# Fourier mixing and a SoLU layer on one core: the down products of two units' signs as seven block products

## The chip, the core and the metric

The kernel runs on one core of a Trainium2 chip. The core has a matrix engine, TensorE (PE in the profile; PEld is its loading of weights), a vector engine (DVE), a scalar engine for activation functions (ACT), a general engine (POOL, GpSimd) and a queue engine that issues transfers (SP). They run side by side and wait for each other by semaphores. PE writes its results to PSUM, which has eight banks; all other data lie in SBUF. All data are 32-bit floats, and each such matmul shows in the profile as two passes, each with its own load of weights.

The metric is the time of one execution in device microseconds. The profile is of one execution.

## The reference

```python
X = np.fft.fft(x, axis=1)            # x: (8, 3136, 256)
X = np.fft.fft(X, axis=2)
x = X.real.reshape(25088, 256)

h = x @ w_in                          # (25088, 1024)
e = np.exp(h - max(h))                # by row
solu = h * e / (sum(e) + 1e-9)
ln = (solu - mean(solu)) / np.sqrt(var(solu) + 1e-6) * g_ln
out = ln @ w_out                      # (25088, 256)
```

## The kernel before

**Units.** The sequence transform of length 3136 = 49 x 64 is done in two stages. Two batches make a pair, so there are four pairs; k1 runs over 25 of the 49 frequencies of the first stage, since the others are mirrors. A unit (L214) is one k1 of one pair, 128 tokens, and with it their 128 mirror tokens: these are its two signs. Units with k1 = 0 have one sign. There are 100 units, 96 of them with two.

**A step** of the loop (L617) begins unit i and ends unit i - 4 (`lag`). It issues, for unit i: `up` (L222), two matmuls of 512 columns for the even and two for the odd part of h; `even` (L230, DVE) adds the middle term to the even part; `join` (L236, DVE) makes h of sign 0 from the even and the odd part, then h of sign 1 from h of sign 0, each with its row maximum; `expo` (L245, ACT) the exponentials u; `product` (L254, DVE) u times h; `square` (L261, ACT) the sum of squares about the mean; `turn_blocks` (L290, DVE) transposes u by blocks of 32; `stats` (L268, POOL) the factor rs of each token from the variance. Every second step `move_blocks` (L312) issues 16 transfers on the SP queue, which place the blocks of two units so that uT is their full transpose. The buffers of uT are two, each for two units.

For unit i - 4 the step issues `down` (L321), for each sign eight matmuls that add up a 128 x 1024 by 1024 x 256 product in PSUM: the stationary operand is a chunk of uT, whose signs lie alternately in memory, the moving one is 256 columns of Wo. `scale` (L328, ACT) multiplies by rs on the way to SBUF and `store` (L332) writes it out, sign 0 from the SP queue, sign 1 by an indirect transfer of POOL's.

For unit i + 2 it issues `transform2` (L189, PE), `take2` (L203, ACT, a copy to q) and `spread` (L207, SP, one row of q to r).

**The next pair** is prepared in the same steps: `load` (L101, SP and POOL), `add_mirror` (L126, POOL), `fold` (L134, DVE and ACT), `transform1` (L145, PE, then a copy on ACT and a transfer by `keep`, L178, on SP) and `turn` (L181, four transfers on POOL each), which brings a fifth of the pair's k1 back in another layout. `START` (L494) says in which steps; the transforms come at k1 from 4 to 19, the turns at 20 to 24. The last pair's steps have none of these.

**Order.** Every instruction stands on its engine's queue in the order in which the program issues it (`manual_schedule`, L519); no scheduler moves it. The first four units (`whole`) are transposed on PE instead (L295). PSUM holds two tiles of two banks each for `up` and four banks, taken in turn under one tag (`ps_m`, L77), for everything else.

Of the kernel before, what the change touches and what calls it, by code (L numbers as in the profile page):

```python
# [35 lines left out]
def kernel(  # L36
# [34 lines left out]
    gpool = ctx.enter_context(tc.tile_pool(name="gpool", bufs=6))  # L71
# [5 lines left out]
    ps_m = ctx.enter_context(tc.tile_pool(name="ps_m", bufs=4, space=PSUM))  # L77
# [5 lines left out]
    Wo = const.tile([P, KF, D], FP32, name="Wo")  # L83
    ones = const.tile([P, P], FP32, name="ones")
# [7 lines left out]

    class Pair:
        def __init__(self, p):
            self.p = p
            self.raw, self.y, self.y0 = {}, {}, None
            self.g, self.zs = {}, {}
# [45 lines left out]
    def transform1(pr, s):  # L145
# [6 lines left out]
        if l == 0:  # L152

            if pr.p or c < 2:
                pr.z = zpool.tile([ZR, CH, D], FP32, tag="z", name="z")
            elif c < 4:
                z = fpool.tile([P, FF], FP32, tag="u", name="z_u", bufs=2)
                pr.z = z[0:ZR].rearrange("p (l d) -> p l d", l=CH)
            else:
                pr.z = gpool.tile([P, KG, D], FP32, tag="g", name="z_g")[0:ZR, 0:CH, :]  # L160
            pr.zs[c] = pr.z
        y = pr.y[c]
        ps = ps_m.tile([P, 2, D], FP32, tag="m", name="ps1")
        if s == NH // 2 - 1:
            parts = [(ps[0:ZR, 0], y[:, l], 0), (ps[0:ZR, 1], pr.y0[:, 0], 1), (ps[0:ZR, 1], y[:, l + 1], 2)]
        else:
            parts = [(ps[0:ZR], y[:, l : l + 2], 0)]
        first = True
# [20 lines left out]
    def transform2(pr, k1):  # L189
# [6 lines left out]
        ps = ps_m.tile([P, KD * P], FP32, tag="m", name="ps2")  # L196
# [39 lines left out]
    def join(t, ps):  # L236

        t.nmax = small.tile([P, 2], FP32, tag="nmax", name="nmax")
        for s in t.signs:
            t.h[s] = fpool.tile([P, FF], FP32, tag="h", name="h", bufs=2)  # L240
            nc.vector.tensor_tensor_reduce(out=t.h[s], in0=t.h[0] if s else t.ev, in1=ps,  # L241
                                           scale=1.0 if s else -0.5, scalar=-3.0e38, op0=ALU.add, op1=ALU.max,
                                           accum_out=t.nmax[:, s : s + 1])

    def expo(t):  # L245
        t.esum = small.tile([P, 2], FP32, tag="esum", name="esum")
        t.neg = small.tile([P, 2], FP32, tag="neg", name="neg")
        for s in t.signs:
            nc.scalar.mul(out=t.neg[:, s : s + 1], in_=t.nmax[:, s : s + 1], mul=-1.0)  # L249
            t.u[s] = fpool.tile([P, FF], FP32, tag="u", name="u", bufs=2)  # L250
            nc.scalar.activation(out=t.u[s], in_=t.h[s], func=ACT.Exp, bias=t.neg[:, s : s + 1],  # L251
                                 accum_out=t.esum[:, s : s + 1])
# [15 lines left out]
    def stats(t):  # L268

        n = slice(0, len(t.signs))  # L270
        es = small.tile([P, 2], FP32, tag="es", name="es")
        nc.gpsimd.tensor_scalar(out=es[:, n], in0=t.esum[:, n], scalar1=1e-9, scalar2=1e-3,  # L272
                                op0=ALU.add, op1=ALU.mult)
        es2 = small.tile([P, 2], FP32, tag="es2", name="es2")
        nc.gpsimd.tensor_tensor(out=es2[:, n], in0=es[:, n], in1=es[:, n], op=ALU.mult)
        v = small.tile([P, 2], FP32, tag="v", name="v")
        nc.gpsimd.tensor_scalar(out=v[:, n], in0=t.ssq[:, n], scalar1=float(FF) ** -3, scalar2=None, op0=ALU.mult)  # L277
        nc.gpsimd.tensor_tensor(out=v[:, n], in0=v[:, n], in1=es2[:, n], op=ALU.add)
# [16 lines left out]
    def turn_whole(t):  # L295
# [4 lines left out]
        for s in t.signs:  # L300
            for half in range(2):
                ps = ps_m.tile([P, n, P], FP32, tag="m", name="ps_t")
# [17 lines left out]

    def down(t, s):  # L321
        uT = t.batch.uT[:, t.w].rearrange("p c i (n s) -> p c (i n) s", s=2)
        ps = ps_m.tile([P, D], FP32, tag="m", name="ps_o")
# [28 lines left out]
    mantissa = const.tile([P, NW], I32, name="mantissa")  # L352
    limits = const.tile([P, 3], FP32, name="limits")
# [12 lines left out]
    def exponent(w, raw):  # L366
# [3 lines left out]
        unit = qpool.tile([P, NW], I32, tag="unit", name="unit", bufs=3)  # L370
# [38 lines left out]
    class Weights:  # L409
# [72 lines left out]
        def centre(self):  # L482

            cs = ps_m.tile([P, D], FP32, tag="m", name="cs")
# [25 lines left out]
    def ahead_pe(pr, step):  # L510
# [5 lines left out]
        if 0 <= step - 20 < NK // KG:  # L516
            turn(pr, step - 20)

    with tc.manual_schedule():  # L519
# [24 lines left out]
        for i, limit in enumerate((-896.0, 255.0, 255.0 * 2.0 ** 23)):  # L544
            nc.vector.memset(limits[:, i : i + 1], limit)
# [56 lines left out]
        def begin(i):  # L602

            cur = units[i]
            if i % 2 == 0:
                batches.append(Batch(i >= whole))
            cur.batch, cur.w = batches[-1], i % 2
            even(cur, up(cur, 0))
            cur.odd = up(cur, 1)
            if i + 2 < len(units):  # L610
                nxt = units[i + 2]
                take2(nxt, transform2(pairs[nxt.p], nxt.k1))
                spread(nxt)
# [3 lines left out]
        for i in range(len(units) + lag):  # L617
            cur = units[i] if i < len(units) else None
            old = units[i - lag] if i >= lag else None
            ahd = pairs[cur.p + 1] if cur and cur.p + 1 < NP else None  # L620
            last = i >= len(units) - 2
            prv = units[i - 1] if 0 < i <= whole else None
            if i > lag:
                store(units[i - lag - 1])
            if cur and i > whole:
                begin(i)
            if prv:
                turn_whole(prv)
            if cur:
                join(cur, cur.odd)  # L630
# [3 lines left out]
            if cur:  # L634
                expo(cur)
            if ahd:
                ahead_pe(ahd, cur.k1)
            if old:
                order = old.signs[::-1] if old is units[-1] else old.signs
                ps_o = [down(old, s) for s in order]  # L640
            if i == 0:

                weights.narrow_out(3)
            if cur:
                for s in cur.signs:
                    product(cur, s)
                    if i < whole and s == 0:
                        square(cur, s)
                if i == 1:
                    weights.centre()  # L650
                if i < whole:

                    begin(i + 1)
                for s in cur.signs:
                    if i >= whole or s:
                        square(cur, s)
                    if i >= whole:
                        turn_blocks(cur, s)
            if old:
                scale(old, order[0], ps_o[0])  # L660
            if cur:
                if last:
                    move_blocks(batches[-1], slice(cur.w, cur.w + 1), (nc.sync, nc.gpsimd) if cur.w else (nc.sync,))
                elif cur.w and i >= whole:
                    move_blocks(batches[-1], slice(0, 2))
                stats(cur)
            if i == 0:
                turn(first, 1, nc.sync)
            elif i in (5, 8, 11):
                turn(first, (i + 1) // 3)  # L670
            if ahd:
                ahead(ahd, cur.k1)
            if old and 1 in old.signs:
                scale(old, order[1], ps_o[1])
        store(units[-1])
# [76 lines left out]
```

## Time and profile before

| | |
|---|---|
| time, three runs | 1188.86, 1189.22, 1191.11 us; median 1189.22 |
| profiled execution | 1191.11 us, its span 1189.0 us |
| granted TensorE clock | 1.000 of full |
| down products, L325 | 3136 passes of 128x256, mean 379 ns; 56% of the chain |
| up products, L227 | 800 passes of 128x512, mean 593 ns; 28% of the chain |
| second transform, L199 | 400 passes of 128x128, mean 274 ns; 4% of the chain |
| weight loads of L325, L199 | mean 196 and 191 ns |
| DMA | 16 engines, mean 156 GB/s |
| SP: 16 moves of uT (L319), every second step | 128 KB each |

How to read it: the profile's times of single matmuls include a tail that the next one overlaps, so their pitch is read from the chain of waits or from a group's length. The page's chain follows the work that ended last back from the end of the kernel; its shares say which engine's work was on that path. In a timeline the first column is the start from the beginning of the span, the second the length, and brackets give the idle time of the engine before the instruction and what ended it. In a list of groups the numbers behind the bar are the busy time of all, the mean of one in ns, and the idle time before them. Lines of a helper can stand for many places.

### The profile page before, as it was taken

How to read it: one execution, taken by the hardware profiler on the slowest of the kernel's cores; microseconds unless marked ns; L12 is line 12 of the kernel's file. 1: busy time of each engine (PE TensorE's matmuls, PEld its weight loads, DVE VectorE, ACT ScalarE, POOL GpSimd, SP SyncE). 2: the span in 40 equal slices, each digit the busy share in tenths (PEclk: the TensorE clock that was granted, in tenths of full speed). 3: DMA queues.
4: the chain of work that ended last, by engine and by line, in shares of the span. 5: the costliest groups of instructions: out<-in, count | busy, mean ns of one | idle time of the engine just before them, and what ended most of it. 6: DMA issues, size and time to landing. Idle time of an engine off the chain costs nothing.

```text
span 1189.0 us, 15738 instructions
## 1 busy us (share of the span) xinstructions
PE 1152.6 (97%) x4720; PEld 874.5 (74%) x4720; DVE 912.3 (77%) x1234; ACT 679.9 (57%) x1404; POOL 505.9 (43%) x766
## 2 busy tenths in 40 slices
PE   2989999999999999999999999999999999999998
PEld 1556777778777777777777777777777777777787
DVE  6879777777768877787778978777786887877780
ACT  3566665656546656565556656565564665655561
POOL 3025556444544444442644554443553333333323
PEclk9999999999999999999999999999999999999999
DMA  9671989958996766655996887775897464554544
GB/s 231 199 188 27 191 187 193 196 138 165 176 168 165 178 168 167 164 137 140 175 176 170 176 170 166 160 165 133 152 187 142 108 154 97 137 122 116 135 104 117
DMA packets 458452, 185.37 MB, mean 156 GB/s; under 512 B 425750, under 2 KB 440350, under 8 KB 458368
## 3 DMA queue, kind: packets, MB, share of 16 engines
q1 hardware_dynamic: 444608, 146.22, 58.3%
q0 software_dynamic: 13760, 38.16, 12.9%
q8 instruction: 38, 0.62, 0.2%
q14 instruction: 46, 0.38, 0.1%
HBM read 44.78 MB, written 38.80 MB: 70 GB/s over the span
## 4 chain that ended last, share of the span: by engine, by line
PE 93%; DMA 3%; DVE 2%; SPq 1%; issue 1%; POOL 1%; ACT 0%; DVEq 0%; ACTq 0%; POOLq 0%
PE ps_o L325 56%; PE ps_h L227 28%; PE ps L171 5%; PE ps L199 4%; DMA raw_in<-in_moe_w_in_dram 2%; PE wps L456 1%; DMA r<-q 1%; SPq L179 1%; DVE h L241 0%; POOL uT L319 0%; DMA out_dram<-ot,idx 0%; DVE y L123 0%; SPq L442 0%; PE ps_t L305 0%; DVE xa L131 0%
## 5 line engine op out<-in xcount | busy, mean ns | idle before, releaser
L325 PE MATMUL ps_o<-Wo,uT 128*128 128x256 f32 x3136 | 693.4, 379 | 1.3 <-ACT uT L310 0.9
L325 PEld LDWEIGHTS ps_o<-Wo,uT 128*128 128x128 f32 x3136 | 610.8, 196 | 64.0 <-ACT uT L310 1.1
L227 PE MATMUL ps_h<-Wi,q 128*128 128x512 f32 x800 | 360.5, 593 | 5.1 <-DVE ev L233 3.0
L272 POOL TENSOR_SCALAR es<-esum 128x2 f32<-128x2 f32 (+1 forms) x100 | 116.4, 1164 | 425.3 <-ACT u L251 425.1
L258 DVE SCALAR_TENSOR_TENSOR u<-h,u 128x1024 f32<-128x1024 f32 x196 | 239.9, 1225 | 33.5 <-ACT u L251 20.7
L227 PEld LDWEIGHTS ps_h<-Wi,q 128*128 128x128 f32 x800 | 151.5, 190 | 154.3 <-issue 142.3
L265 ACT ACTIVATE h<-u,usum 128x1024 f32<-128x1024 f32 x196 | 224.5, 1147 | 14.8 <-DVE u L258 9.0
L233 DVE SCALAR_TENSOR_TENSOR ev<-w_mid,r,ps_h 128x1024 f32<-128x1024 f32 x100 | 127.8, 1278 | 135.0 <-PE ps_h L227 127.1
L251 ACT ACTIVATE u<-h,neg 128x1024 f32<-128x1024 f32 x196 | 225.6, 1151 | 6.4
L293 DVE STREAM_TRANSPOSE v<-u 128x1024 f32<-128x1024 f32 x192 | 227.5, 1224 | 0.1
L205 ACT COPY q<-ps 128x256 f32<-128x256 f32 x100 | 37.1, 372 | 306.7 <-PE ps L199 279.5
L241 DVE CUSTOM_DVE_ANT_0 h<-ev,ps_h 128x1024 f32<-128x1024 f32 x100 | 122.1, 1221 | 48.9 <-PE ps_h L227 45.3
L330 ACT ACTIVATE ot<-ps_o,rs 128x256 f32<-128x256 f32 x196 | 90.6, 465 | 75.3 <-PE ps_o L325 66.3
L241 DVE CUSTOM_DVE_ANT_0 h<-h,ps_h 128x1024 f32<-128x1024 f32 x96 | 117.3, 1222 | 14.2 <-ACT neg L249 0.5
L337 POOL DMA_INDIRECT out_dram<-ot,idx x96 | 103.1, 1074 | 41.9 <-issue 21.4
L171 PE MATMUL ps<-y,F 98*100 98x258 f32 (+3 forms) x288 | 72.5, 389 | 25.2 <-DVE y L124 25.2
L199 PEld LDWEIGHTS ps<-T,g 128*128 128x128 f32 x400 | 60.2, 191 | 47.4 <-issue 46.9
L249 ACT ACTIVATE neg<-nmax 128x1 f32<-128x1 f32 x196 | 38.8, 198 | 71.0 <-DVE nmax L241 70.9
L280 POOL TENSOR_TENSOR rs<-v,neg_half 128x2 f32<-128x2 f32 (+1 forms) x100 | 71.7, 717 | 7.8
L171 PEld LDWEIGHTS ps<-y,F 98*100 98x100 f32 x288 | 46.3, 179 | 37.6 <-DVE y L124 24.3
L277 POOL TENSOR_SCALAR v<-ssq 128x2 f32<-128x2 f32 (+1 forms) x100 | 22.9, 229 | 117.7 <-ACT h L265 117.6
L199 PE MATMUL ps<-T,g 128*128 128x128 f32 x400 | 60.6, 274 | 0.0
(72 smaller groups left out, 493.9 us busy)
## 6 DMA issues: line engine op xcount, KB each, us to landing
uT<-v SPq DMA_DIRECT2D x752, 128.0 KB
out_dram<-ot SPq DMA_DIRECT2D x100, 128.0 KB
g<-zd POOLq DMA_DIRECT2D x72, 160.0 KB, 5.5
xa<-in_x_dram SPq DMA_DIRECT2D x28, 392.0 KB
zd<-z SPq DMA_DIRECT2D x24, 400.0 KB
raw_in<-in_moe_w_in_dram SPq DMA_DIRECT2D x4, 512.0 KB
raw_out<-in_moe_w_out_dram SPq DMA_DIRECT2D x2, 1024.0 KB
r<-q SPq DMA_DIRECT2D x100, 0.5 KB
```

What stands on the lines that cost most here:

```text
L171: nc.tensor.matmul(o[..., cs], F[:, 2 * t + h, :], i[..., cs], start=first, stop=True, skip_group_check=True)
L199: nc.tensor.matmul(o, g[:, k, h * P : (h + 1) * P], table, start=(h == 0), stop=True, skip_group_check=True)
L227: nc.tensor.matmul(ps[:, fs], t.q[:, c * P : (c + 1) * P], Wi[:, c, fs], start=True, stop=True)
L233: nc.vector.scalar_tensor_tensor(out=t.ev, in0=w_mid, scalar=t.r, in1=ps, op0=ALU.mult, op1=ALU.add)
L241: nc.vector.tensor_tensor_reduce(out=t.h[s], in0=t.h[0] if s else t.ev, in1=ps, scale=1.0 if s else -0.5, scalar=-3.0e38, op0=ALU.add, op1 ...
L251: nc.scalar.activation(out=t.u[s], in_=t.h[s], func=ACT.Exp, bias=t.neg[:, s : s + 1], accum_out=t.esum[:, s : s + 1])
L258: nc.vector.scalar_tensor_tensor(out=t.u[s], in0=t.h[s], scalar=1.0, in1=t.u[s], op0=ALU.mult, op1=ALU.mult, accum_out=t.usum[:, s : s + 1])
L265: nc.scalar.activation(out=t.h[s], in_=t.u[s], func=ACT.Square, bias=t.usum[:, s : s + 1], scale=-float(FF), accum_out=t.ssq[:, s : s + 1])
L272: nc.gpsimd.tensor_scalar(out=es[:, n], in0=t.esum[:, n], scalar1=1e-9, scalar2=1e-3, op0=ALU.add, op1=ALU.mult)
L293: nc.vector.transpose(out=t.batch.v[:, t.w, :, o], in_=t.u[s])
L325: nc.tensor.matmul(ps, uT[:, c, :, s], Wo[:, c, :], start=(c == 0), stop=(c == KF - 1))
L337: dma = nc.gpsimd.indirect_dma_start(out=out, out_offset=bass.IndirectOffsetOnAxis(ap=idx[:, i : i + 1], axis=0), in_=t.ot[s], in_offset=None)
```

## The change

For units with two signs, but for the last unit, the product of the 2 x 2 blocks (two signs by two halves of the 1024 features) with the 2 x 2 blocks of Wo (two halves of the features by two halves of the 256 outputs) is no longer made as eight block products, but as seven (Strassen's scheme in Winograd's form). A block product is four matmuls of 128 columns with new weights each.

- The four differences of Wo's blocks are made once (`weight_sums`, POOL). The four sums and differences of u's blocks are made by POOL for each unit one step ahead (`sums`), one of them in place in uT.
- `Down` issues the seven products into three PSUM banks. Three intermediate results are copied by ACT, one of them from bank to bank so that PE adds to it; two results are finished by DVE (`sum22`, `sum12`) from PSUM and a copy. The seventh product, p4, and the scales of three of the four output blocks stand in the next step. There are four scales of 128 columns, in place of two of 256.
- The squares and `stats` of a unit move to the head of the next step, and all of `stats` but the last power goes from POOL to ACT.
- `join` and `expo` are issued for each sign by itself, and the seven products stand between the other PE work of the step: up 0, p4 of the unit before, p1, first transform, p5, up 1, p6, p2, second transform, p7, p3.
- PSUM's four single banks have fixed uses: the two transforms share one, `Down` has three. The buffers of g go from six to three, and the pairs' `turn` steps from 20 to 24 of the pair before to -5, -3, 2, 6 and 11 of the pair's own count. Rooms in SBUF that the first pair borrows change with it.
- `store` stands after p5. Units with one sign, and the last unit, go on with `down`.

```diff
-    gpool = ctx.enter_context(tc.tile_pool(name="gpool", bufs=6))
+    gpool = ctx.enter_context(tc.tile_pool(name="gpool", bufs=3))
-    ps_m = ctx.enter_context(tc.tile_pool(name="ps_m", bufs=4, space=PSUM))
+    spool = ctx.enter_context(tc.tile_pool(name="spool", bufs=2))
+    ps_m = ctx.enter_context(tc.tile_pool(name="ps_m", bufs=1, space=PSUM))
...
+    Ws = const.tile([P, 4, KF // 2, P], FP32, name="Ws")
...
+    def result(i):
+        return ps_m.tile([P, 2 * D], FP32, tag=f"m{i % 4}", name="ps_m")
...
-        ps = ps_m.tile([P, 2, D], FP32, tag="m", name="ps1")
+        ps = result(0 if pr.p else s).rearrange("p (l d) -> p l d", l=2)
...
-        ps = ps_m.tile([P, KD * P], FP32, tag="m", name="ps2")
+        ps = result(0)[:, 0 : KD * P]
...
     def stats(t):
         n = slice(0, len(t.signs))
-        es = small.tile([P, 2], FP32, tag="es", name="es")
-        nc.gpsimd.tensor_scalar(out=es[:, n], in0=t.esum[:, n], scalar1=1e-9, scalar2=1e-3,
-                                op0=ALU.add, op1=ALU.mult)
-        es2 = small.tile([P, 2], FP32, tag="es2", name="es2")
-        nc.gpsimd.tensor_tensor(out=es2[:, n], in0=es[:, n], in1=es[:, n], op=ALU.mult)
-        v = small.tile([P, 2], FP32, tag="v", name="v")
-        nc.gpsimd.tensor_scalar(out=v[:, n], in0=t.ssq[:, n], scalar1=float(FF) ** -3, scalar2=None, op0=ALU.mult)
-        nc.gpsimd.tensor_tensor(out=v[:, n], in0=v[:, n], in1=es2[:, n], op=ALU.add)
+        es2, v = (small.tile([P, 2], FP32, tag=tag, name=tag) for tag in ("es2", "v"))
+        nc.scalar.activation(out=es2[:, n], in_=t.esum[:, n], func=ACT.Square, bias=limits[:, 3:4], scale=1e-3)
+        for s in t.signs:
+            nc.scalar.activation(out=v[:, s : s + 1], in_=t.ssq[:, s : s + 1], func=ACT.Identity, bias=es2[:, s : s + 1],
+                                 scale=float(FF) ** -3)
         t.rs = small.tile([P, 2], FP32, tag="rs", name="rs")
         nc.gpsimd.tensor_tensor(out=t.rs[:, n], in0=v[:, n], in1=neg_half[:, n], op=ALU.pow)
...
+    def weight_sums():
+        B11, B12, B21, B22 = [Wo[:, k : k + KF // 2, f : f + P] for k in (0, KF // 2) for f in (0, P)]
+        for j, (a, b) in enumerate(((B12, B11), (B22, Ws[:, 0]), (B22, B12), (B21, Ws[:, 1]))):
+            nc.gpsimd.tensor_tensor(out=Ws[:, j], in0=a, in1=b, op=ALU.subtract)
+
+    def blocks(t):
+        uT = t.batch.uT[:, t.w].rearrange("p c i (n s) -> p s c (i n)", s=2)
+        return [uT[:, s, c : c + KF // 2] for s in range(2) for c in (0, KF // 2)]
+
+    def sums(t):
+        A11, A12, A21, A22 = blocks(t)
+        t.S = spool.tile([P, 3, KF // 2, P], FP32, tag="S", name="S")
+        for o, a, b, op in ((t.S[:, 0], A21, A22, ALU.add), (t.S[:, 1], t.S[:, 0], A11, ALU.subtract),
+                            (A21, A11, A21, ALU.subtract), (t.S[:, 2], A12, t.S[:, 1], ALU.subtract)):
+            nc.gpsimd.tensor_tensor(out=o, in0=a, in1=b, op=op)
+
+    def product7(o, a, b, start=False):
+        n = KF // 2
+        for c in range(n):
+            nc.tensor.matmul(o, a[:, c], b[:, c], start=start and c == 0, stop=c == n - 1, skip_group_check=True)
...
+    class Down:
+        def __init__(self, t, fresh):
+            self.t = t
+            self.C11, self.C21, self.P53 = (bank(i)[:, 0:P] for i in range(3))
+            self.E5, self.X, self.C12, self.C22 = (
+                small.tile([P, P], FP32, tag=f"E{i}", name=f"E{i}", bufs=2) for i in range(4))
+            self.A11, self.A12, self.S3, self.A22 = blocks(t)
...
+        def p1(self):
+            product7(self.C11, self.A11, Wo[:, 0 : KF // 2, 0:P], True)
+            nc.scalar.copy(self.C21, self.C11)
+        def p5(self):
+            product7(self.P53, self.t.S[:, 0], Ws[:, 0], True)
+            nc.scalar.copy(self.E5, self.P53)
+        def p6(self):
+            product7(self.C21, self.t.S[:, 1], Ws[:, 1])
+            nc.scalar.copy(self.X, self.C21)
+        def p2(self):
+            product7(self.C11, self.A12, Wo[:, KF // 2 :, 0:P])
+            self.scale(0, 0, self.C11)
+        def p7_p3(self):
+            product7(self.C21, self.S3, Ws[:, 2])
+            product7(self.P53, self.t.S[:, 2], Wo[:, KF // 2 :, P:])
+        def sum22(self):
+            nc.vector.tensor_tensor(out=self.C22, in0=self.C21, in1=self.E5, op=ALU.add)
+        def sum12(self):
+            nc.vector.tensor_tensor(out=self.C12, in0=self.P53, in1=self.X, op=ALU.add)
+        def p4(self):
+            product7(self.C21, self.A22, Ws[:, 3])
+            self.scale(0, 1, self.C12)
+            self.scale(1, 1, self.C22)
+            self.scale(1, 0, self.C21)
+        def scale(self, s, half, ps):
+            nc.scalar.mul(out=self.t.ot[s][:, half * P : (half + 1) * P], in_=ps, mul=self.t.rs[:, s : s + 1])
...
-        if 0 <= step - 20 < NK // KG:
-            turn(pr, step - 20)
+
+    def turn_parts(pr, step):
+        if step in (-5, -3, 2, 6, 11):
+            turn(pr, (-5, -3, 2, 6, 11).index(step))
...
+        for i in range(whole + 1, len(units) + lag + 1):
...
+            if prv:
+                for s in prv.signs:
+                    square(prv, s)
+                stats(prv)
+            if nxt and len(nxt.signs) == 2:
+                sums(nxt)
+            if cur:
+                enter(i)
+                ps = up(cur, 0)
+            if half:
+                half.p4()
+                half = None
+            seven = old and len(old.signs) == 2 and old is not units[-1]
+            if seven:
+                half = Down(old, i == whole + 1)
+                half.p1()
+            if cur:
+                other_pairs(i, ahead_pe)
+                even(cur, ps)
+            if seven:
+                half.p5()
...
+            store(units[i - lag - 1])
+            if cur:
+                cur.odd = up(cur, 1)
+                join(cur, 0)
+            if seven:
+                half.p6()
+            if cur:
+                expo(cur, 0)
+            if seven:
+                half.p2()
...
+            if cur:
+                second_transform(i + 2)
+                if 1 in cur.signs:
+                    join(cur, 1)
+                    expo(cur, 1)
+            if seven:
+                half.p7_p3()
+            if cur:
+                product(cur, 0)
+            if seven:
+                half.sum22()
+            if cur and 1 in cur.signs:
+                product(cur, 1)
+            if seven:
+                half.sum12()
+            if cur:
+                for s in cur.signs:
+                    turn_blocks(cur, s)
...
+                for pr in pairs[1:]:
+                    turn_parts(pr, i - pr.p * NK)
+                other_pairs(i, ahead)
```

## The prediction

> **What bounds the kernel now.** I read the page's shares and its chain first, then the chain in order of time in mid-run, then one step of all engines.
>
> ```profile
> PE 1152.6 (97%) x4720; PEld 874.5 (74%) x4720; DVE 912.3 (77%) x1234; ACT 679.9 (57%) x1404; POOL 505.9 (43%) x766
> PE 93%; DMA 3%; DVE 2%; SPq 1%; issue 1%; POOL 1%; ACT 0%; DVEq 0%; ACTq 0%; POOLq 0%
> ```
>
> PE works for 97% of the span and is 93% of the chain. One step of that chain, from the chain of waits between 700 and 760 us:
>
> ```profile
> 702.10 6.91 PE ps_o L325 x32
> 709.01 3.43 PE ps_h L227 x8
> 712.44 0.44 PE ps L199 x4
> 712.88 0.87 PE ps L171 x4
> ```
>
> A step is 6.91 (both down products) + 3.43 (up) + 0.44 (second transform) = 10.8 us, and 11.65 with the first transform's 0.87. PE never waits, so every other engine's time is cover. How much is the question, for the change spends it. From the timeline of the same step:
>
> ```profile
> 700.92 1.22 DVE L241 CUSTOM_DVE_ANT_0 h<-ev,ps_h 128x1024 f32<-128x1024 f32 x1 [0.53 <-PE ps_h L227]
> 702.18 0.20 ACT L249 ACTIVATE neg<-nmax 128x1 f32<-128x1 f32 x1 [0.54 <-DVE nmax L241]
> 702.42 1.15 ACT L251 ACTIVATE u<-h,neg 128x1024 f32<-128x1024 f32 x1
> 703.48 0.19 ACT L251 ACTIVATION_READ_ACCUMULATOR u<-h,neg 128x1 f32 x1
> 703.70 1.23 DVE L258 SCALAR_TENSOR_TENSOR u<-h,u 128x1024 f32<-128x1024 f32 x1 [0.17 <-ACT u L251]
> 705.07 1.22 DVE L258 SCALAR_TENSOR_TENSOR u<-h,u 128x1024 f32<-128x1024 f32 x1
> 705.13 1.22 POOL L272 TENSOR_SCALAR es<-esum 128x2 f32<-128x2 f32 x1 [4.71 <-ACT u L251]
> 706.22 2.37 DVE L293 STREAM_TRANSPOSE v<-u 128x1024 f32<-128x1024 f32 x2
> ```
>
> DVE starts h at 700.92 and ends the transposes at 708.59; with the 1.28 of ev (L233) its loop is under 9 us of the step. POOL's es starts 0.06 after a product and ends with it.
>
> **The change part by part.** *Down products.* Out: 32 passes of 256 columns, 6.91 us. In: 7 products x 4 chunks x 2 passes = 56 passes of 128 columns, each with new weights. The nearest row is the second transform: four such passes in 0.44, 0.11 each, though its weights are read contiguously and half of the new ones with a stride of two. That stride costs a weight load 196 instead of 191 ns today (L325 against L199), so the pitch lies between 0.111 and 0.117; I take 0.111. 56 x 0.111 = 6.2, a gain of 0.68 a step, 65 us over the 95 units that use it. PE's step becomes 10.1, or 10.97 with the first transform.
>
> The Trainium skill (TensorE: Matmul & The Clock Gate, Back-to-back issue gap) speaks against this: in a stream of weight loads and matmuls it gives 81 ns at 128 columns where the matmul alone takes 56. As an estimate from that page, 0.111 would become 0.16, the 56 passes 9.0 us, and the sum 200 us slower; the row above, a stream of this kind at 0.11, decides.
>
> *ACT.* A copy of 256 columns takes 0.372 (L205), of 512 0.567 (L174): 0.28 for 128. A scale of 256 takes 0.465 (L330), 0.09 over the copy: 0.37 for 128, up to 0.396 (L448). New per step: three copies 0.83, four scales for two +0.6, and es2 and two v at 0.2 (as L249) 0.6: ACT goes from 57% to some 71%. That is covered, but for two that stand between the two exponentials: the scale after p2 and the copy of q, 0.74.
>
> *DVE.* sum22 and sum12, 0.29 each: the row for 98x127 is 0.279 (L122). Nothing is removed.
>
> *The DVE-ACT loop*, which each unit passes before the next can: h to first product 2.78 (700.92 to 703.70); to the second product 0.74 + neg 0.24 + exponential 1.06 + readout 0.19 after the first readout's end at 703.67, so 2.23; second product 1.15 and sum12 0.29; transposes 2.37; ev 1.28. Together 10.1 us, which is PE's new step without the first transform. A fold (L122, L123) adds 1.27 every second step, so 10.7 against 10.97 where the first transform runs. The cover that was over 2 us a step is now 0 to 0.3.
>
> *POOL.* Out: es 1.17, es2 0.22, v 0.23 and 0.20. In: four sums of 512 columns. A tensor_tensor takes 2.34 for 1020 columns and 1.80 undisturbed for 765, so 2.1 ns a column and 1.26 for 512: 5.0 us a step. POOL with rs, stores, gathers and mirror sums then has 18.5 us per two steps of 21.9. The first sum waits for uT to land, and behind it queue the store, L131's mirror sum, the gather, turn and the next rs; DVE's folds and ACT's scales need those one to three steps later.
>
> *Moves.* Squares and variance go to the head of the next step, rs is used three steps later: nothing. turn, 20 DMAs a pair at 0.607, is as often on POOL, later; each part is needed five or more steps on: nothing. The SP queue issues the same:
>
> ```profile
> 697.39 13.83 SPq L319 DMA_DIRECT2D uT<-v  x16
> ```
>
> with POOL's uT pieces landing 2.9 us after issue, about 16.5 in all. It now starts when the transposes end, 4.8 us into the next step, and lands 21.3 us after that step began, 10.4 into the one after; uT is first needed by a sum there, and by PE one step later. Covered by about 5 us, except after the short steps of k1 = 0, where I charge 4 us twice.
>
> *Costs at the edges.* PE's short steps (8.2, 8.2 and 7.3 us) can no longer be absorbed by a 10.1 loop: +7. Two steps with two first transforms wait for one PSUM bank, whose copy stands behind the squares and scales on ACT: +2 each. The drain keeps three units of seven products, and the sums queue behind the last POOL moves: 0. Weight sums: 4 x 1.26 on an idle POOL in step 1: 0.
>
> *The port.* What DVE and POOL do to each other is the term that decides:
>
> ```profile
> L272 POOL TENSOR_SCALAR es<-esum 128x2 f32<-128x2 f32 x96 | 112.6, 1172 | 403.3 <-ACT u L251 403.1
> L275 POOL TENSOR_TENSOR es<-es 128x2 f32<-128x2 f32 x96 | 21.3, 222 | 8.1
> 240.31 0.68 DVE L123 TENSOR_TENSOR y<-xa 98x508 f32<-98x508 f32 x1
> 240.36 2.30 POOL L131 TENSOR_TENSOR xa<-xa,xb 98x765 f32<-98x765 f32 x1
> L131 POOL TENSOR_TENSOR xa<-xa,xb 98x765 f32<-98x765 f32 x3 | 5.9, 1965 | 0.0
> ```
>
> The 1172 against 222 ns is POOL waiting out a DVE product with two SBUF inputs; the mirror sum beside a fold took 2.30 where the other two of its kind took 1.80 (5.9 less 2.30, halved). No row has POOL first and such a DVE operation second for long: today they never meet so. The price per product is thus between 0 (a fold that started 0.06 after rs still took 0.68, but rs reads two columns) and a whole sum, 1.26. I take that who comes first keeps the port, as the es row has it from the other side: half a sum, 0.63, on two products of three, since the sums start 10.4 us into a step and the products 9.7 and 11.9, and in the other step they follow rs. That is 0.85 a step, plus 0.3 for a fold in every second. Loop: 10.95 without the first transform (before 10.8, +0.16 x 47) and 11.85 with it (before 11.65, +0.2 x 48).
>
> The skill's page SBUF — State Buffer, Who interferes with whom, says that whichever of the two starts first holds the port for its whole instruction. Without that rule's second half my sum would be that of the first rival; with it, that of the forecast. No run shows it yet.
>
> Sum: 7.5 + 9.6 + 7 + 4 + 8 = +36 on the span of 1189.0, with 2.1 outside it in the profiled execution of 1191.1; its time lies 1.9 over the median of 1189.2, from which I count: **1226 us**. The 65 us of PE work saved become waits.
>
> **The rivals.** *The port is not held against DVE*: then DVE's loop is 10.1 and 10.7, PE stays the bound: -65 + 7 + 4 + 8 + 9 (loop and step equal where there is no transform, 0.2 x 47 for their jitter) = -37, 1152 us. For it: PE's dense chain and the fold beside rs; against: the es row. *Weight loads do not overlap*, 0.196 a pass: 56 x 0.196 = 11.0, +4.1 x 95, 1576 us; the L199 row is against it. *POOL becomes the bound*: its 18.5 us per two steps plus up to 4.9 of waiting out four products, 23.4 against 21.9, and the sums reach PE late whenever the uT burst stretches: 12.2 to 12.4 a step on 95, where the mean before was 11.2, 1290 us. It decides once POOL's idle time before the uT landing no longer fits; the page's 43% today is for it only if the waits add up.
>
> **How the numbers follow.** Forecast 0.56, port free 0.37, POOL 0.06, weight loads 0.01. The forecast's own range, from one product in two meeting a sum to every product doing so (+0.4 a step), is 1205 to 1255; with the port-free case the range is 1148 to 1255. Under 0.2% a measurement here cannot tell from nothing. Faster 0.35 (nearly all of the port-free case), the same 0.03, slower 0.62.
>
> **What would show it.** PE's passes of the seven products at 0.11; sums at 1.26 or more on POOL; DVE's products longer than 1.23 or preceded by idle time while a sum runs; PE idle before up and down with DVE or POOL as the releaser, and a share well under 97%. Wrong if products keep 1.23 beside running sums: then it is the port-free case. If PE is dense and the passes are long, it is the weight loads.

## The result and the profile after

The changed kernel takes 1312.99 us (median of four runs, 1307.94 to 1320.03) beside 1190.16 us before on the same chip: ratio 1.104, 95% interval 1.098 to 1.110. The profiled execution took 1309.26 us, its span 1307.4. The direction of the prediction is right; the size is not: 1226 was said, with a range that ended at 1255.

The page of the kernel after, busy time of each engine, the chain's shares, and the granted clock in 40 slices:

```profile
PE 1175.4 (90%) x7002; PEld 918.2 (70%) x7002; DVE 1045.8 (80%) x1425; ACT 840.2 (64%) x2175; POOL 930.7 (71%) x750
PE 28%; DVE 19%; DMA 16%; SPq 14%; issue 10%; ACT 9%; POOL 4%; DVEq 0%; ACTq 0%; POOLq 0%
PEclk9999999989998999999999989998999999999999
```

PE was 93% of the chain and is 28%: the chain now wanders over DVE, the moves of uT and SP's queue. PE's busy time did not fall at all, though its passes are fewer in work; and the clock has slices at 8, where before it had none. (9 stands for 90% or more; the mean over the span is 0.964.)

The groups of instructions of the kernel after, shapes kept apart:

```profile
L268 DVE SCALAR_TENSOR_TENSOR u<-h,u 128x1024 f32<-128x1024 f32 x196 | 330.2, 1686 | 41.5 <-ACT u L261 40.6
L350 POOL TENSOR_TENSOR S<-S,uT 128x512 f32<-128x512 f32 x95 | 149.7, 1575 | 7.5
L182 PE MATMUL ps_m<-y,F 98*100 98x258 f32 x120 | 42.8, 442 | 80.3 <-ACT ps_m L383 44.4 <-DVE y L130 23.8 <-DVE y L128 9.9
```

A product takes 1.69 us on average against 1.23 in the step shown of before; a sum of this kind takes 1.58, not 1.26. And the first transform, which PE entered without a wait in the step shown of before, has 80 us of idle time ahead of it. The 24 of them that wait for L130 lie in the first pair, at the start of the kernel; the kernel before has 25 there.

The timeline of a step that waits for a fold. PE's step begins with `up` at 513.43, while DVE is still at the products of the step before:

```profile
513.43 1.88 PE L238 MATMUL ps_h<-Wi,q 128*128 128x512 f32 x4
513.47 2.02 POOL L350 TENSOR_TENSOR uT<-uT 128x512 f32<-128x512 f32 x1
514.73 1.85 DVE L268 SCALAR_TENSOR_TENSOR u<-h,u 128x1024 f32<-128x1024 f32 x1
515.46 2.28 POOL L350 TENSOR_TENSOR S<-uT,S 128x512 f32<-128x512 f32 x1
516.09 1.11 PE L355 MATMUL ps_m<-Wo,uT 128*128 128x128 f32 x8
516.71 2.35 DVE L300 STREAM_TRANSPOSE v<-u 128x1024 f32<-128x1024 f32 x2
519.00 0.64 DVE L128 TENSOR_TENSOR y<-xa 98x508 f32<-98x508 f32 x1
519.56 0.67 DVE L129 TENSOR_TENSOR y<-xa 98x508 f32<-98x508 f32 x1
519.78 1.18 PE L182 MATMUL ps_m<-y,F 98*100 98x258 f32 x4 [2.59 <-ACT ps_m L383]
520.79 1.50 PE L355 MATMUL ps_m<-Ws,S 128*128 128x128 f32 x8
522.08 3.16 PE L238 MATMUL ps_h<-Wi,q 128*128 128x512 f32 x4
```

The product at 514.73 is held back by the sum that runs to 515.49, the next sum by the product. p1, the eight passes at 516.09, is done at 517.2. The first transform is next in PE's queue and needs the fold. DVE still has the transposes before it; the first part of the fold, L128, ends at 519.64, and 0.14 us later the transform starts. (The brackets name ACT's copy at L383, which ended 0.04 us after L128; it feeds no operand of the transform. In run 7 below this copy ended a whole us before the transform in several steps, and the transform still began 0.15 us after L128, as in every wait of this kind.) After the wait PE itself is slow: four passes of 512 columns at L238 take 3.16 us, where in other steps they take 1.88. In the table of stretches of the same kernel (busy time of PE, PEld, DVE, ACT, POOL with counts, granted clock, DMA share, GB/s):

```profile
517.80:521.20 3.40, 1.42 (x8) 1.10 (x9) 3.40 (x5) 2.02 (x9) 3.28 (x5) 1.00 0.75 158
521.20:524.60 3.40, 3.40 (x9) 1.89 (x9) 0.22 (x1) 0.65 (x2) 1.94 (x3) 0.51 1.05 232
```

PE was busy for 1.42 us of the first stretch, and in the next its clock was halved. The clock record has 27 such windows of 3.41 us in the kernel after and, but for the very end, none in the one before; 27 x 3.41 / 2 = 46 us.

Step lengths, from the start of one even `up` to the next in the trace: the mean of 30 steps in two stretches with folds and first transforms (T), of 17 steps at the end, which have neither (Q), and the smallest of each kind.

| | T | Q | smallest T, Q |
|---|---|---|---|
| before | 11.63 | 10.79 | 11.65, 10.79 |
| after | 13.45 | 10.78 | 11.19, 10.32 |
| predicted | 11.85 | 10.95 | PE: 10.97, 10.1 |

(Before and after, the 30 steps take in two without a first transform, so the mean lies below 11.65 in the kernel before.) So the time was lost in the T steps: 1.82 us each, 82 us over some 45 of them, of 118 in all. It isn't spread evenly: in the second pair the steps run 16.39, 11.44, 15.79, 11.22, 16.25, 11.22 us and so on, the long ones being those whose transform needs the fold of the step before. 8.5 us more are the drain after the last `up` (50.9 us against 42.4). 17 us are the two steps that end a unit with k1 = 0 and wait for a fold as well (17.65 and 15.73 us against 8.20). The rest are single steps of 12 to 16 us, some of them near a turn.

### The profile page after: what moved, and what is told of

Read it like the earlier page. It is cut to its first block, busy times and chain, and to the rows that moved or that the text cites. A ratio compares the mean times of both kernels' runs of the same rounds, so it can differ in the third digit from the quotient of the medians.

```text
span 1307.4 us, 21623 instructions
## 1 busy us (share of the span) xinstructions
PE 1175.4 (90%) x7002; PEld 918.2 (70%) x7002; DVE 1045.8 (80%) x1425; ACT 840.2 (64%) x2175; POOL 930.7 (71%) x750
## 4 chain that ended last, share of the span: by engine, by line
PE 28%; DVE 19%; DMA 16%; SPq 14%; issue 10%; ACT 9%; POOL 4%; DVEq 0%; ACTq 0%; POOLq 0%
SPq L326 14%; PE ps_m L355 13%; PE ps_h L238 9%; DMA uT<-v 8%; DVE u L268 6%; DVE v L300 5%; DMA out_dram<-ot 3%; DVE h L252 3%; ACT h L275 2%; ACT u L261 2%; PE ps_m L182 2%; POOL S L350 2%; DMA room<-in_x_dram 2%; PE ps_m L421 1%; DVE y L129 1%
## 5 line engine op out<-in xcount | busy, mean ns | idle before, releaser
L238 PE MATMUL ps_h<-Wi,q 128*128 128x512 f32 x800 | 393.3, 616 | 0.8 <-DVE nmax L252 0.8
L350 POOL TENSOR_TENSOR S<-uT 128x512 f32<-128x512 f32 x95 | 150.6, 1586 | 173.6 <-DMA r<-q 71.9
L355 PEld LDWEIGHTS ps_m<-Ws,S 128*128 128x128 f32 x1520 | 206.5, 203 | 74.5 <-issue 46.7
L355 PEld LDWEIGHTS ps_m<-Ws,uT 128*128 128x128 f32 x1520 | 200.4, 196 | 48.8 <-issue 28.9
L355 PE MATMUL ps_m<-Ws,S 128*128 128x128 f32 x1520 | 219.1, 291 | 12.6 <-POOL S L350 7.2
L355 PE MATMUL ps_m<-Wo,uT 128*128 128x128 f32 x1520 | 212.4, 283 | 15.0 <-issue 3.6
L238 PEld LDWEIGHTS ps_h<-Wi,q 128*128 128x128 f32 x800 | 145.6, 202 | 107.9 <-issue 105.1
L355 PE MATMUL ps_m<-Ws,uT 128*128 128x128 f32 x1520 | 210.9, 282 | 2.3 <-DVE E L402 2.3
L355 PEld LDWEIGHTS ps_m<-Wo,uT 128*128 128x128 f32 x1520 | 195.5, 197 | 18.4 <-ACT ot L414 4.2
L350 POOL TENSOR_TENSOR S<-S,uT 128x512 f32<-128x512 f32 x95 | 149.7, 1575 | 7.5
L350 POOL TENSOR_TENSOR S<-uT,S 128x512 f32<-128x512 f32 x95 | 148.7, 1565 | 0.0
L350 POOL TENSOR_TENSOR uT<-uT 128x512 f32<-128x512 f32 x95 | 137.7, 1450 | 0.0
L244 DVE SCALAR_TENSOR_TENSOR ev<-w_mid,r,ps_h 128x1024 f32<-128x1024 f32 x100 | 124.8, 1248 | 5.3 <-DMA r<-q 3.7
```

The lines of the kernel that those rows point to most:

```text
L238: nc.tensor.matmul(ps[:, fs], t.q[:, c * P : (c + 1) * P], Wi[:, c, fs], start=True, stop=True)
L244: nc.vector.scalar_tensor_tensor(out=t.ev, in0=w_mid, scalar=t.r, in1=ps, op0=ALU.mult, op1=ALU.add)
L350: nc.gpsimd.tensor_tensor(out=o, in0=a, in1=b, op=op)
L355: nc.tensor.matmul(o, a[:, c], b[:, c], start=start and c == 0, stop=c == n - 1, skip_group_check=True)
```

## The experiments

Two theories stood against each other. A: PE's order is wrong by one step for the first transform, and its waits halve the clock on top. B: the meetings of DVE and POOL at the port lengthen DVE's loop, and the late fold is only where it shows. The first three runs vary both, alone and together.

**1. First transform one step later** (with the turns shifted so that they still follow it).

```diff
-                if step == START[pr.p == 1][c] + 2 + half:
+                if step == START[pr.p == 1][c] + 3 + half:
...
-        if step in (-5, -3, 2, 6, 11):
+        if step in (-4, -3, 2, 6, 11):
```

> The first transform of a piece is issued one step later, so that the fold it reads is a whole step old; the sums on POOL stay. Theory A (the fold, made late by the DVE loop and the port, holds PE in its own queue at the first transform, and the matrix clock drops after each such gap): the 74 us in which PE waits ahead of the first transform go, and most of the 26 half-clock windows (44 us) with them: about 1200 us (1185 to 1220), granted clock 0.99 or more. Theory B (the DVE loop itself, lengthened by the port, is the bound, and PE's wait at the transform is only where it shows): the wait moves to the up products, 1280 us or more.

1248.31 us, ratio 1.049 [1.045, 1.053], clock 0.985, T 11.95. A gain of 65 us, less than A alone asks and more than B allows. PE's idle time ahead of the transforms is gone after the start; what is left shows in the timeline of this kernel:

```profile
524.59 1.28 POOL L350 TENSOR_TENSOR S<-S,uT 128x512 f32<-128x512 f32 x1
524.75 2.20 DVE L268 SCALAR_TENSOR_TENSOR u<-h,u 128x1024 f32<-128x1024 f32 x1 [0.17 <-ACT u L261]
525.83 2.02 POOL L350 TENSOR_TENSOR uT<-uT 128x512 f32<-128x512 f32 x1
526.88 0.28 DVE L402 TENSOR_TENSOR E<-ps_m,E 128x128 f32<-128x128 f32 x1
527.22 1.21 PE L355 MATMUL ps_m<-Ws,uT 128*128 128x128 f32 x8 [1.84 <-DVE E L402]
```

The product waits out the sum that runs to 525.87 and holds up the next, sum22 stands behind the product in DVE's queue, and p4 on PE waits for sum22, since it adds to that bank. This is the loop of DVE as the bound, which the prediction meant.

**2. No sums** (the products read blocks of uT in place of S).

```diff
-        t.S = spool.tile([P, 3, KF // 2, P], FP32, tag="S", name="S")
-        for o, a, b, op in (...):
-            nc.gpsimd.tensor_tensor(out=o, in0=a, in1=b, op=op)
+        t.S = (A22, A11, A12)
```

> The four sums of each unit on POOL are left out (the seven products read blocks of uT in their place), so nothing on POOL meets DVE's products; the order of issue stays. Theory A: the order alone leaves some 2 us of wait at the first transform in each of 24 fold steps, about 45 us, and part of the clock windows; 1225 to 1250 us. Theory B: without port waits the loop fits, 1150 to 1170 us.

1224.32 us, ratio 1.030 [1.028, 1.033], clock 0.994, T 12.23. The groups of this kernel:

```profile
L268 DVE SCALAR_TENSOR_TENSOR u<-h,u 128x1024 f32<-128x1024 f32 x196 | 244.0, 1246 | 62.4 <-ACT u L261 62.3
L182 PE MATMUL ps_m<-y,F 98*100 98x258 f32 x120 | 41.5, 429 | 60.3 <-ACT ps_m L380 31.2 <-DVE y L130 22.1 <-DVE y L128 5.0
```

The products are back at 1.25 us, and PE still waits 60 us ahead of the transform, 38 of them beyond the first pair's: the late fold is a cause of its own, without any meeting at the port.

**3. Both.**

> Both edits: the first transform one step later and no sums on POOL. Both theories: PE is dense again at 10.97 us a step with the first transform and 10.1 to 10.3 without, 1140 to 1160 us. Later than 1180 would mean that a third cost (the ACT chain, the landing of uT) is missing from both.

1189.35 us, ratio 1.000 [0.999, 1.002], clock 0.999, T 11.49, Q 10.62. The two causes, taken out together, give 124 us. The order is worth 65 us with sums and 35 without; the sums 89 with the old order and 59 with the later one. They overlap, since a product held back makes the fold later still. But it is not the 1140 to 1160 that was expected: something third was missing (run 12).

**4. The sums put into the kernel before**, where nothing reads them.

> The kernel before, with four sums of 512 columns a unit added on POOL whose results nobody reads (one buffer of g less makes room). If the port costs time only where DVE has no cover: DVE's products go from 1.23 to 1.5 us or more, yet PE stays at 97% and the time within 1% of 1190. If the port's waits cost wherever they occur: 2 products x 0.5 us x 96, 95 us, 1285 us.

1217.01 us, ratio 1.022 [1.021, 1.024]; T 11.82, Q 10.79. The product in this kernel's groups:

```profile
L259 DVE SCALAR_TENSOR_TENSOR u<-h,u 128x1024 f32<-128x1024 f32 x196 | 310.4, 1595 | 29.4 <-ACT u L252 22.0
```

Its mean is 0.37 us over the 1225 ns of the kernel before, and in most steps nothing follows from that: 10.79 us to the hundredth without a first transform, and mostly 11.65 with one. Yet the time is 27 us longer, more than the 1% of the first expectation and far less than the second's 95. The 27 lie in a few single steps of 12 to 17 us and, some 6 of them, at the start and in the drain; what makes those steps long isn't shown. (This kernel also has one buffer of g less.) So the same sums cost 27 us where DVE's loop had about 2 us to spare, and 59 to 89 where it had none.

**5 and 6. h kept in PSUM**, so that a product has one operand in SBUF and one in PSUM; with the old order (5) and the later transform (6).

```diff
-        t.h[s] = fpool.tile([P, FF], FP32, tag="h", name="h", bufs=2)
-        ...(out=t.h[s], in0=t.h[0] if s else t.ev, in1=t.odd, scale=1.0 if s else -0.5, ..., op0=ALU.add, ...)
+        t.h[s] = t.odd if s else t.even
+        ...(out=t.h[s], in0=t.ev, in1=t.odd, scale=-0.5, ..., op0=ALU.subtract if s else ALU.add, ...)
```

> h of both signs stays in the PSUM tiles of up, so that a product reads one operand from SBUF and one from PSUM; sums, passes and order are those of the kernel after. Theory A (the sums cost what they hold back DVE's products, through the port that both read SBUF by): products return to 1.15 to 1.25 us beside running sums and POOL's sums to 1.3, only the folds still meet them. What is left is the late first transform and PE's half clock: 1205 to 1240 us, near the kernel without sums less its 14 us of slower passes. Rival B (the sums cost by coming late to PE, the port matters little): time stays above 1275 us though the products are short.

> As the run before, and the first transforms one step later with the turns moved to match. Theory A (order and port are the two causes, and the pass pitch of 0.118 us where uT is the weight explains the rest): dense steps of 10.32 us without and 11.19 us with the first transform, 1160 to 1195 us, that is at or below the kernel before. Rival B (POOL, late with its sums, is a cause of its own): over 1225 us, with PE waiting at p5, p6 or p3 for a sum.

1284.64 us, ratio 1.081 [1.076, 1.086], and 1240.64 us, ratio 1.044 [1.042, 1.045]. By the times alone both speak for B. The groups and the waits of run 6 say otherwise (waits: us in total, times, the longest):

```profile
L268 DVE SCALAR_TENSOR_TENSOR u<-ps_h,u 128x1024 f32<-128x1024 f32 x196 | 240.1, 1225 | 78.4 <-ACT u L261 77.9
L351 POOL TENSOR_TENSOR S<-S,uT 128x512 f32<-128x512 f32 x95 | 125.1, 1316 | 7.4
```

```profile
PE ps_h L238 <- DVE u L268: 38.7, 19, 4.8
PE ps_m L356 <- POOL S L351: 3.5, 3, 2.9
```

Products and sums run side by side at 1.23 and 1.32 us: with an operand in PSUM there is no meeting. PE hardly waits for sums, so rival B falls. But `up` now waits for the product that still reads its PSUM tile, and the smallest steps are 10.65 and 11.46 us, not 10.32 and 11.19. The edit took away one wait and made another; the price of the port can't be read from these two times. Run 5 has the late fold besides: PE waits 40 us ahead of the transform beyond the first pair's.

**7. PE kept at work while it waits**: eight matmuls into the transform's bank, which it then overwrites.

```diff
+        if pr.p and l == 0:
+            for k in range(8):
+                nc.tensor.matmul(ps[:, 0, 0:P], ident, Wo[:, 0, 0:P], start=True, stop=True, skip_group_check=True)
```

> The kernel after with 16 more passes (1.8 us, of ident and Wo, into the bank that the first transform overwrites) ahead of every first transform that waits for its fold: 384 passes, 42 us of PE work that change no result. Theory A (the halved clock follows PE's idle stretches of 2 us and over and costs some 40 us by itself): the extra passes lie in the idle time, windows at half clock fall from 26 to under 8, and the time falls by 20 to 40 us, to 1270 to 1292 us. Rival B (the clock is not what idle time does, or the windows cost nothing since DVE sets the step): 1309 us or up to 1330, the extra passes adding where the wait was shorter.

1287.28 us, ratio 1.085 [1.082, 1.087], clock 0.988, windows at half clock 9 (27 in the kernel after; "26" above was a miscount). 42 us of useless work made the kernel 26 us faster. So the halved clock has a price of its own: 18 windows fewer are 31 of its 46 us by the sum above, and 26 us came off the time.

**8. Seven products only in steps without folds and transforms.**

> Seven products only for the about 49 units that are ended in steps without the next pair's folds, mirror sums and first transforms; all others by the two down products of the kernel before; the first transforms one step later, the turns moved to match. Theory A (DVE and POOL have no room for the folds, the mirror sums and u's four sums in one step; where they stand apart, PE sets the pace): 10.32 to 10.5 us in the quiet steps against 10.79 before, 11.65 in the others as before, so 0.3 to 0.47 x 49 less and some 10 us more for the edges: 1172 to 1188 us, faster than before. Rival B (the sums and the longer chain to p4 cost in the quiet steps too, as the outliers of 13 to 16 us there in the kernel after): 1195 us or more.

1344.03 us, ratio 1.129 [1.125, 1.133]. A flaw of the edit, seen in the waits of this kernel:

```profile
PE ps_m L182 <- ACT q L216: 80.5, 46, 2.1
```

The two transforms share one bank. In a step with the old `down` the copy of the second transform stands on ACT behind an exponential and two scales that need the end of PE's step; the next first transform waits for it, and all such steps take 13.65 us. So the time says nothing on what such a mix is worth. The quiet steps at the end say something: they took 10.86 us on average, not the 10.32 to 10.5 of theory A, so beside the sums the seven products gain nothing there on average.

**9. Only sign 1's h in PSUM**, later transform. The odd tile is written next 4.5 us or more into the following step, so `up` seldom waits for the product (three times, 9.8 us in all).

> As the run with the first transforms later (1248), but h of sign 1 alone stays in the PSUM tile of up's odd part, which is next written 4 us into the following step. Theory A (the port's price stands on DVE's loop, 0.46 us for each of two products): one product of two at 1.23 us, no new wait of PE for it, 1205 to 1230 us. Rival B (POOL's lateness, not the products' length, sets what is left): 1238 to 1250.

1221.23 us, ratio 1.026 [1.023, 1.029], T 11.53, Q 10.50; 27 us less than run 1. The groups of this kernel have the experiment in two lines:

```profile
L268 DVE SCALAR_TENSOR_TENSOR u<-h,u 128x1024 f32<-128x1024 f32 x100 | 163.4, 1634 | 28.4 <-ACT u L261 28.4
L268 DVE SCALAR_TENSOR_TENSOR u<-ps_h,u 128x1024 f32<-128x1024 f32 x96 | 117.0, 1219 | 22.7 <-ACT u L261 22.1
```

Beside the same sums the product with both operands in SBUF takes 1.63 us, the one with an operand in PSUM 1.22. It isn't the place in the step: in run 1 sign 1's product, with both operands in SBUF, took 1.73.

**10. Sums made and not read** (order of run 1, products as in run 3).

> As the run with later transforms and no sums (1189), but POOL makes the four sums of each unit again, into SBUF, and nothing reads them (the products read blocks of uT). The port is used as in the kernel after, but PE never waits for a sum. Theory A (what the sums cost is DVE's time at the port): at or over the run with sums in use, 1240 to 1262 us, since its passes are 14 us slower. Rival B (the cost is PE's wait for late sums): under 1210 us. Between 1215 and 1235 both share.

1249.54 us, ratio 1.052 [1.047, 1.057]. PE cannot wait for a sum here, and yet the sums cost 60 us against run 3. The product in this kernel's groups:

```profile
L268 DVE SCALAR_TENSOR_TENSOR u<-h,u 128x1024 f32<-128x1024 f32 x196 | 352.9, 1802 | 41.1 <-ACT u L261 40.6
```

And PE's longest wait in total, for sum22 (2.1 us in run 3):

```profile
PE ps_m L356 <- DVE E L403: 23.7, 22, 1.9
```

So what the sums cost is not their own lateness; they cost without being waited for. That DVE's time at the port is the price is shown by run 9, 27 us for one product of two, and by this wait for an operation that stands behind a product. What the sums cost by holding up POOL's other work was not taken apart from it.

**11. Turns between two bursts of moves** (run 9 with the turns behind the sums of odd steps). In run 9's timeline a turn, issued in the midst of a burst, is followed by a step of 15.65 us:

```profile
326.84 3.88 SPq L327 DMA_DIRECT2D uT<-v  x4
328.41 2.34 POOL L198 DMA_DIRECT2D g<-zd  x4
337.84 0.83 PE L356 MATMUL ps_m<-Wo,uT 128*128 128x128 f32 x5 [2.73 <-DMA uT<-v]
```

The last of the burst was issued by 330.7, and p1 is let go at 337.8, 7 us later; the sums wait as well.

> The run with later transforms and h of sign 1 in PSUM (1221), with each turn issued by POOL right behind the sums of an odd step, when a burst of 16 moves has just landed and the next is half a step away, not at the end of a step in the midst of one. Theory A (the steps of 14 to 18 us that follow a turn are PE and POOL waiting for uT, whose moves share the DMA engines with the turn's 1.3 MB): the waits of p1 for uT fall from 19 us to under 6, 1180 to 1205 us. Rival B (these steps have another cause, such as the short steps of k1 = 0): 1212 us or more.

1227.10 us, ratio 1.029 [1.026, 1.033]: no gain, as rival B's "1212 us or more" has it. (A turn is 4 x 160 KB, half of the 1.3 MB written above.) The step of 15.65 became 10.64, another of 15.74 became 10.99, and PE's idle time ahead of p1 and p2 fell from 18 to 11 us. In exchange one turn came too late; from the waits:

```profile
PE ps_m L210 <- DMA g<-zd: 5.3, 1, 5.3
```

That the turns delay uT is thus seen in single steps; that it is worth anything in sum was not shown.

**12. Weights from neighbouring columns** (run 3 with another view of uT).

```diff
-        uT = t.batch.uT[:, t.w].rearrange("p c i (n s) -> p s c (i n)", s=2)
+        uT = t.batch.uT[:, t.w].rearrange("p c i m -> p (c i m)").rearrange("p (s c k) -> p s c k", s=2, c=KF)
```

> The run with later transforms and no sums (1189), its products reading 128 neighbouring columns of uT as weights instead of every second one of 256: the same passes, other values. Theory A (what that run lost against the kernel before's 1190 less 65 is for its larger part the pass pitch, 0.118 us with a stride of two against 0.112): 56 x 0.006 = 0.34 us less in each of 95 steps, dense steps of 10.13 us, 1155 to 1167 us. Rival B (the loop of DVE and ACT, 10.1 us by my sum with no meeting at the port, or the landing of uT sets the step as soon as PE is quicker): 1175 us or more, steps staying at 10.4.

1175.38 us, ratio 0.987 [0.985, 0.989], with smallest steps of 10.13 and 11.00 us instead of 10.46 and 11.32. In the kernel after both kinds of weights stand side by side; from its timeline:

```profile
509.28 1.05 PE L355 MATMUL ps_m<-Ws,S 128*128 128x128 f32 x8
510.17 1.12 PE L355 MATMUL ps_m<-Wo,uT 128*128 128x128 f32 x8
511.13 0.61 PE L210 MATMUL ps_m<-T,g 128*128 128x128 f32 x4
```

Eight passes with S as weights take 0.89 us from start to start, with uT 0.96: 0.111 and 0.120 a pass; the medians over the kernel are 0.112 and 0.118. The pitch is the third cost, as A has it, but only 14 of the 32 us came back: PE, now quicker, waits more (37 us in gaps over 0.3 us from 60 us on, 27 in run 3). Of theory A the steps held to the hundredth, 10.13, and the time did not; of rival B the time held by 0.4 us, and the steps did not.

## Why the prediction was right and wrong, point by point

- *PE's gain, 0.68 us a step and 65 in all.* Mis-sized: the smallest steps show 10.79 - 10.32 = 0.47, 45 us. The text had the bounds, "between 0.111 and 0.117; I take 0.111", but 32 of the 56 passes of a step have uT as weights, and these run at 0.118. The 0.16 a pass that the text set aside is not seen here.
- *The port.* "who comes first keeps the port": right, and both ways. The price of 0.85 us a step for two products was 2 x (1.69 - 1.23) = 0.92. The Trainium skill (SBUF — State Buffer, Who interferes with whom) adds that a DVE instruction with at most one SBUF input, outside DVE's 2-port modes, does not contend with GpSimd; runs 6 and 9 agree (1.23 and 1.22 us beside running sums).
- *DVE's loop where no transform runs, 10.95.* The 17 steps at the end took 10.78, their smallest 10.32: most of them lost nothing. A held-back product is made good in part, it seems, by a later step in which the sums come at another time; no run shows that by itself.
- *The step with the first transform, 11.85.* This is the step that failed: "so 10.7 against 10.97 where the first transform runs". It averaged the fold over two steps and weighed DVE's loop against PE's length, as if a buffer of steps lay between. I had placed the transform in the list of PE's work and had written that the folds are needed "one to three steps later", but did not ask when in that step. It stands right behind p1, some 3.5 us into the step after the fold's, and the fold ends over 6 us into it. The text had the figures for this: it lets the transposes end "4.8 us into the next step", and the fold stands behind them on DVE, so it ends at 6.1. PE, which runs in order, passes the wait on to all that stands behind it: 2.6 us in the step shown, and 13.45 us for T in place of 11.85. Where the order is mended (run 1) T is 11.95, and the time, 1248, lies within the forecast's own 1205 to 1255. So the term of the port was near, though this is a mean of steps from 11.19 to 14.88 us, and the order took the other 65 us.
- *What no step had:* the clock. A wait of 2.6 us costs up to another 1.7 behind it (half of 3.41). By run 7 some 26 us at least are its price.
- *uT covered "by about 5 us", turns "nothing".* The cover fails where a turn's transfers run beside a burst, as in run 9's step of 15.65 us. The drain, set at 0, is 8.5.
- *The sum.* Its terms add up to 1225, not 1226, and it counts a fold's 0.3 us at the port, due in every second step, in all 48 steps, some 7 us too many. Neither matters beside the 65.
- *The rivals.* With the port free and the order right (run 3) the time is 1189, not 1152: the pitch takes 14 of the 37 us between them (run 12) and the drain 3 (45.3 us against 42.4); the rest, PE's gaps in single steps, was not taken apart. POOL as the bound, by sums that reach PE late, is out: PE waits 7 us in all for them in the kernel after, and run 10 costs as much without any such wait. That its 1290 was the figure nearest to the result is chance. Long weight loads are out, since the passes run at 0.112 and 0.118.

No version with the seven products and the whole computation beats the kernel before; the nearest is run 9 at 1221 us.

## What to carry to other kernels

Before work is spent from a cover, look at the in-order queue that stands behind it: not "is the loop shorter than the step on average" but "when in the step is this result asked for, and what stands behind the asker". A fold that is due one step later can be due at once. And where DVE and POOL share work in SBUF, giving one operand of the DVE instruction a place in PSUM removes their meeting (1.22 us here in place of 1.63), if the PSUM tile is not asked for soon.

## What the runs showed of the hardware

**The port is kept by whoever starts, in both directions.** From the timeline of the kernel after, at a mirror sum:

```profile
719.51 2.39 POOL L137 TENSOR_TENSOR xa<-xa,xb 98x1020 f32<-98x1020 f32 x1
720.47 2.52 DVE L268 SCALAR_TENSOR_TENSOR u<-h,u 128x1024 f32<-128x1024 f32 x1 [0.17 <-ACT u L261]
721.82 1.24 POOL L138 TENSOR_TENSOR xa<-xa,xb 98x4 f32<-98x4 f32 x1
```

The product waits out the mirror sum to 721.9 and then runs; the sum of four columns, 0.21 us elsewhere, waits out the product to 723.0.

**PE's clock halves after a stretch that was about half idle.** In a trace all windows at half clock begin on one grid of 3.413 us. In the fourteen traces, from 60 us on, each window of this grid at full clock, by the time that PE was busy in it by the profile, and how often the next window was at half clock:

| PE busy in a window of 3.41 us | windows | next one at half clock |
|---|---|---|
| under 1.5 us | 98 | 98 |
| 1.5 to 1.9 us | 73 | 22 |
| over 1.9 us | 4528 | 0 |

So a wait of some 2 us costs clock when it falls into one window.

The Trainium skill (TensorE: Matmul & The Clock Gate, What's actually happening) speaks of free-running windows of 3413 ns, and of the half clock after at least one idle window. The length of the window and the fixed grid agree. But a whole idle window is not needed: PE was busy for 1.42 of the 3.40 us that came before the halved window shown above, and for up to 1.8 us in others.

**Weights with a stride of two cost 0.006 us a pass** of 128 columns (0.118 against 0.112; run 12 has 0.112 from the same tile without the stride), and a single weight load takes 196 ns with it and 192 without, at the median of the kernel after. How 4 ns of an overlapped load become 6 ns of pitch isn't shown.
